# Block-sorted attention and a bilinear feed-forward on one core: Sinkhorn of one batch by itself, Strassen blocks in the out matmul, and a fixed order of work

## The chip, the core and the metric

The kernel runs on one core of a Trainium2 chip. The core has five engines that run side by side, each with its own list of instructions in a fixed order: TensorE (PE, matmuls into PSUM banks), VectorE (DVE), ScalarE (ACT), GpSimd (POOL, which also starts the loads from device memory) and SyncE (SP, which starts stores, transposing transfers and copies through device memory). They wait for one another by semaphores. The metric is device time in microseconds (us) for one execution. Next to it stands the span of a profiled execution, from the first to the last instruction of the core.

## What is computed

There are 4 batches of 8 heads, 768 positions in 8 blocks of 96, head size 64. A small 8x8 matrix per head is normalised five times (exponent, rows, columns; Sinkhorn). It mixes the blocks of k and of v. Attention is then within each block, and its output goes through a bilinear feed-forward: two matrices 512x1536, an elementwise product, a third matrix 1536x512.

```python
P = sort_net                                  # (4, 8, 8, 8)
for _ in range(5):
    P = exp(P - max(P, axis=-1))
    P = P / (sum(P, axis=-1) + 1e-9)
    P = P / (sum(P, axis=-2) + 1e-9)
k_sorted = einsum('bhij,bhjcd->bhicd', P, k_blocks)
v_sorted = einsum('bhij,bhjcd->bhicd', P, v_blocks)
attn = softmax(scale * q_blocks @ k_sorted.T) # inside each block of 96
x = (attn @ v_sorted) as (3072, 512)
out = ((x @ w_a) * (x @ w_b)) @ w_out         # (3072, 512), float32
```

## The kernel before, in words

The matmuls are in bf16 with sums in float32. All work is entered as pieces in a plan (`add` in class `Plan`), each with the engines that may do it, an assumed length, what it depends on, the buffers it takes and returns, and a rank. `solve` walks through assumed time: of the pieces that can begin soonest on an engine it takes the one with the lowest rank, and the result is sorted by assumed start. That sets the order of instructions on each engine for good; on the chip each engine goes through its list and waits where it must.

Two heads make a pair, four pairs a batch. For each pair q is transposed on PE (L473, for batch 3 by a DMA, L625), k and v are mixed with the Sinkhorn matrix on PE (L489, L500 for the halves of batch 0, L537 for v where it goes through device memory, L546 and L550), v is transposed (L559), then scores (L578), exponent on ACT (L583), product with v (L593), division on DVE (L599, L604), and the transposition of the result into `xT` (L612, or a DMA, L620).

The Sinkhorn loop (L413 to L426) works on all 32 heads at once, 32 partitions by 64 numbers: one ACT and six DVE instructions per turn. Its result is repeated 16 times (`p_rep`), transposed by eight small matmuls (L435), and spread with a mask into `s_all` (L440): batch 0 by DVE, the others by POOL. The mixes of a batch wait for its part of `s_all`.

The feed-forward has two stages per batch. The first makes h = (x w_a)(x w_b), transposed. For batch 0 it is plain (L749, 192 matmuls of 384 columns). For batches 1 to 3 it goes by Strassen blocks in Winograd's form (L831): seven products instead of eight, for which POOL and DVE add blocks of the weights (`w_sums`) and of x (`x_sums`), ACT copies a bank between two products that accumulate on it (L840), and DVE or POOL adds and multiplies (L306). The second stage multiplies h by `w_out` (L899): per batch 6 groups of 12 matmuls of 512 columns, each group copied out by ACT (L248) or DVE (L250) and stored by SP (L919). `hT`, `xT` and `tx` exist once; the next batch waits for its readers.

Loads are started by POOL (L350, L362, L379, L387, L406); a load waits for the seventh before it to land. In the beginning PE is kept awake with matmuls on zeros (L983) whose number is worked out from the plan's gaps (`_fill`).

The softmax here doesn't subtract the row's maximum and nothing guards it: scores larger than these inputs give would overflow.

## Time and profile before

| | |
|---|---|
| runs, device time | 245.55, 246.43 and 823.47 us (median 246.43) |
| profiled execution | 245.06 us, span 243.3 us |
| granted TensorE clock | 1.0 |
| matmuls by line, count | L899 288, L831 504, L749 192, L983 48 |
| DMA, mean | 115 GB/s, 27.90 MB; busy from 6 to 62 us nearly without a break |

The page of the profile gives the busy time of each engine, the largest groups of instructions (line, engine, operation, out<-in, partitions x elements, count, busy us, mean ns of one, idle time before it and what ended it), and a chain of work followed back from the last instruction. The chain in order of time shows start, length and what; the timeline shows instructions of one engine, with the idle time before each in brackets. Matmuls overlap, so the spacing of their starts, not the mean length of one, is what one costs in a long run.

### The profile page before, as it was taken

To read this page: it belongs to the slowest core of one execution; us is meant where nothing else is said; L and a number is where in the kernel's file an instruction comes from. 1 tells how busy PE (TensorE), PEld (TensorE's weight loads), DVE (VectorE), ACT (ScalarE), POOL (GpSimd) and SP (SyncE) were. 2 spreads that over 40 slices of the span, in tenths; PEclk is the share of its full clock that TensorE was granted. 3 is DMA by queue.
4 is the path that set the end of the run, shared out by engine and by line. 5 is a ranking of instruction groups with operands and counts; after the bars stand their busy time and mean duration, and the time that the engine had idled before them with its cause. 6 is when DMAs were issued, how large, how long until landed. Compare 5 with 4: busy or idle time off the path is not lost.

```text
span 243.3 us, 5723 instructions
## 1 busy us (share of the span) xinstructions
PE 233.7 (96%) x2204; PEld 132.4 (54%) x2204; DVE 150.1 (62%) x348; ACT 125.3 (52%) x243; POOL 119.6 (49%) x132
## 2 busy tenths in 40 slices
PE   6998999999989999999999999999999999999992
PEld 2466766666655554665544455665654455565440
DVE  6656654654555738589987452988862448886210
ACT  3366646468655533667654443766631076673100
POOL 8979999999970020069755110173540007355000
PEclk9999999999999999999999999999999999999999
DMA  5999999999965683619998867200035450000135
GB/s 67 180 203 187 202 203 187 167 191 178 162 134 107 167 184 78 149 16 154 135 175 110 192 174 178 46 0 0 3 66 108 96 122 0 1 0 3 43 86 129
DMA packets 50106, 27.90 MB, mean 115 GB/s; under 512 B 28832, under 2 KB 47008, under 8 KB 50080
## 3 DMA queue, kind: packets, MB, share of 16 engines
q0 software_dynamic: 24112, 14.16, 43.3%
q1 hardware_dynamic: 25968, 13.38, 25.7%
q8 instruction: 17, 0.28, 0.5%
q14 instruction: 9, 0.07, 0.1%
HBM read 30.29 MB, written 8.26 MB: 158 GB/s over the span
## 4 chain that ended last, share of the span: by engine, by line
PE 67%; ACT 1%; DVE 1%; issue 0%; ACTq 0%; DVEq 0%
PE ps L831 33%; PE ps L899 26%; PE ps L593 2%; PE ps L578 2%; PE ps L489 1%; PE ps L537 1%; PE ps L473 1%; PE ps L749 1%; ACT f L840 0%; DVE xp L604 0%; ACT o L248 0%; DVE a L306 0%; DVE rec L599 0%; ACTq L840 0%; DVEq L306 0%
## 5 line engine op out<-in xcount | busy, mean ns | idle before, releaser
L306 POOL TENSOR_TENSOR hT<-a,f 128x384 bf16<-128x384 bf16 x39 | 35.5, 918 | 78.1 <-DVE f L306 56.3
L899 PE MATMUL ps<-w_out_sb,hT 128*128 128x512 bf16 x288 | 66.4, 379 | 0.0
L840 ACT COPY f<-ps 128x384 f32<-128x384 f32 x108 | 48.2, 482 | 23.6 <-PE ps L831 21.1
L899 PEld LDWEIGHTS <-hT 128*128 128x128 bf16 x288 | 27.0, 98 | 30.1
L306 DVE TENSOR_TENSOR a<-f,ps 128x384 bf16<-128x384 f32 x54 | 29.4, 549 | 10.4 <-PE ps L831 6.4
L306 DVE TENSOR_TENSOR f<-f,ps 128x384 f32<-128x384 f32 x54 | 28.9, 550 | 8.9 <-PE ps L831 6.0
L583 ACT ACTIVATE eT<-ps 96x768 bf16<-96x768 f32 x32 | 24.9, 806 | 17.2 <-PE ps L578 16.9
L306 DVE TENSOR_TENSOR hT<-a,ps 128x384 bf16<-128x384 bf16 x42 | 23.1, 551 | 12.4 <-PE ps L749 6.9
L248 ACT COPY o<-ps 128x512 f32<-128x512 f32 x15 | 8.8, 585 | 36.3 <-PE ps L899 36.3
L831 PE MATMUL ps<-tx,ws_a 128*128 128x384 bf16 x108 | 25.2, 326 | 0.2 <-ACT f L840 0.2
L831 PE MATMUL ps<-tx,ws_b 128*128 128x384 bf16 x108 | 24.9, 326 | 0.3 <-ACT f L840 0.3
L604 DVE TENSOR_TENSOR xp<-ps,rec 96x512 bf16<-96x512 f32 x32 | 21.4, 677 | 0.4
L749 PE MATMUL ps<-xT,w_a_sb 128*128 128x384 bf16 x96 | 19.6, 327 | 0.0
L749 PE MATMUL ps<-xT,w_b_sb 128*128 128x384 bf16 x96 | 19.6, 326 | 0.0
L831 PEld LDWEIGHTS <-ws_b 128*128 128x128 bf16 x144 | 13.8, 98 | 10.1 <-ACT f L840 0.9
L755 ACT CAST a<-ps 128x384 bf16<-128x384 f32 x24 | 11.5, 479 | 14.9 <-PE ps L749 9.1
L250 DVE COPY o<-ps 128x512 f32<-128x512 f32 x9 | 6.2, 691 | 20.8 <-PE ps L899 20.7
L831 PEld LDWEIGHTS <-ws_a 128*128 128x128 bf16 x144 | 13.5, 98 | 10.1 <-ACT f L840 1.4
L831 PE MATMUL ps<-xT,w_b_sb 128*128 128x384 bf16 x72 | 17.6, 326 | 0.3 <-DVE xp L604 0.2
L831 PE MATMUL ps<-xT,w_a_sb 128*128 128x384 bf16 x72 | 17.5, 326 | 0.0
L831 PEld LDWEIGHTS <-w_b_sb 128*128 128x128 bf16 x108 | 10.4, 98 | 7.9 <-DVE xp L604 0.7
L831 PEld LDWEIGHTS <-w_a_sb 128*128 128x128 bf16 x108 | 10.3, 98 | 7.9 <-ACT f L840 0.6
(90 smaller groups left out, 337.9 us busy)
## 6 DMA issues: line engine op xcount, KB each, us to landing
out_dram<-o SPq DMA_DIRECT2D x48, 128.0 KB, 2.4
k<-in_k_dram POOLq DMA_DIRECT2D x16, 192.0 KB, 6.1
v<-in_v_dram POOLq DMA_DIRECT2D x16, 192.0 KB, 6.1
vd<-vm SPq DMA_DIRECT2D x10, 192.0 KB, 2.9
vs<-vd SPq DMA_DIRECT2D x10, 192.0 KB, 3.1
q<-in_q_dram POOLq DMA_DIRECT2D x16, 96.0 KB, 6.9
w_a_sb<-in_moe_w_a_dram POOLq DMA_DIRECT2D x4, 384.0 KB, 7.1
w_b_sb<-in_moe_w_b_dram POOLq DMA_DIRECT2D x4, 384.0 KB, 9.0
```

Of the source, the lines that this page charges most:

```text
L248: nc.scalar.copy(out=out, in_=in_)
L250: eng.tensor_copy(out=out, in_=in_)
L306: ENG[eng].tensor_tensor(out=out, in0=in0, in1=in1, op=op)
L578: nc.tensor.matmul(sc[:, e, i * BLK:(i + 1) * BLK], lhsT=kT[e * D:(e + 1) * D, at:at + P], rhs=rhs, start=True, stop=True)
L583: nc.scalar.activation(out=buf(("eT", b, p, h))[:, :, 0:HB], in_=buf(("sc", b, p, h))[0:BLK, :, 0:HB], func=AF.Exp, scale=float(scale))
L593: nc.tensor.matmul(ops_[:, e, i * OW:(i + 1) * OW], lhsT=eT[:, e, i * BLK:i * BLK + P], rhs=vs[:, h * NBH + i, e * OW:(e + 1) * OW], start ...
L604: nc.vector.tensor_tensor(out=_ap(xp, h * NBH * 2 * D, [[NB * 2 * D, BLK], [D, 2], [2 * D, NBH], [1, D]]), in0=_ap(ops_, 2, [[1024, BLK], ...
L749: nc.tensor.matmul(pf[:, 0:HW], lhsT=w_sb[:, kc, m * P:(m + 1) * P], rhs=buf(("xT", b))[:, kc, t * HW:(t + 1) * HW], start=(kc == 0), stop ...
L755: ea = add("ACT", 0.48, lambda: nc.scalar.copy(out=buf(("a", b, t, m)), in_=buf(("pf", b, t, m, "a"))[:, 0:HW]), [pa], get=[("a", ("a", b, ...
L831: nc.tensor.matmul(buf(key)[:, 0:HW], lhsT=lf(j), rhs=rf(j), start=start and j == 0, stop=j == 1, skip_group_check=not start)
L840: return add("ACT", 0.48, lambda: nc.scalar.copy(out=buf((name, b, g, n)), in_=buf(kA)[:, 0:HW]), [dep], get=[("f", (name, b, g, n))], rank=r)
L899: nc.tensor.matmul(po, lhsT=hT[:, t * 2 + m // G, m % G, c * P:(c + 1) * P], rhs=w_out_sb[:, m, :], start=(m == 0), stop=(m == KO - 1), sk ...
```

## The change

It has five parts.

1. *Sinkhorn of batch 0 by itself.* The 8 heads of batch 0 lie as 64 rows (head and row) of 8 numbers. Row sums are done on TensorE: a float32 matmul against a 0/1 matrix of equal heads (`m_same`) both sums over a head's rows and repeats the sum for each row. The state lies transposed, so that ACT takes the reciprocal of the other sum as its scale, and a turn is one ACT, one PE and three DVE instructions. The last product is laid out so that one matmul (`spread_first`) gives the repeated, transposed matrix. The heads of batches 1 to 3 go through the old loop afterwards (24 partitions), with a lower priority.
2. *Out of batches 2 and 3 by Strassen blocks* (`out_strassen`): three chunks of 128 tokens in each half, seven products of six matmuls of 256 columns each; `o_sums` adds blocks of `w_out` (8 operations, once), 24 sums of blocks of h per batch; ACT copies the accumulating bank three times per chunk, DVE adds four times per chunk and the results are stored. Sums and outputs lie in the buffers of q, k, v, `kT` and `s_all`, free by then. Of the last chunk's stores every second is started by ACT.
3. *Loads in one order.* Each load follows the one entered before it (`ld_i`); q, k, v of batch 0 come first, then the first weight blocks, q's second halves, and the weight blocks 2, 1, 3 instead of 1, 2, 3.
4. *The order of all pieces is given* as a table (`ORDER`, two characters per piece) which `solve` follows in place of its own choice. Assumed lengths and delays in the plan are changed, and POOL and DVE sums are planned as sharing a port.
5. *Weight sums* of the second column block may go to DVE; the filler's zeros lie in a part of `ws_b`.

`PLAIN_G` is 6, equal to `G`, so the feed-forward of batch 0 stays plain.

```diff
+        digits = [c - 35 - (c > 92) for c in ORDER]
+        order = [91 * a + b for a, b in zip(digits[::2], digits[1::2])]
+        def given():
+            op = self.ops[order[done] // 2]
+            e = list(op.alts)[order[done] % 2]
+            return begin(op, e, max(self._when(op), op.ready)), e, op
...
-STRASSEN_OUT = ()
+STRASSEN_OUT = (2, 3)
+PLAIN_G = 6
...
-    warm_sb = const.tile([P, 512], BF16, name="warm_sb")
+    warm_sb = ws_b[:, 3, 1, HW // 2 * 4 - 512:HW // 2 * 4]
...
-        i = add("POOL", 0.72 + many, fn, ds, get=get, rank=rank, lat=0.0)
+        i = add("POOL", 0.72 + many, fn, ds + ld_i[-1:], get=get, rank=rank, lat=0.0)
+        ld_i.append(i)
...
-    for c in range(1, 4):
+    for c in (2, 1, 3):
         load_ab(c)
...
+    def sk_rows():
+        nc.tensor.matmul(buf(bank)[0:HN, NB:2 * NB], lhsT=m_same.rearrange("p h j -> p (h j)"),
+                         rhs=pa[:, 1, :], start=True, stop=True)
...
+    for it in range(4):
+        x = step("ACT", 0.3, lambda it=it: nc.scalar.activation(
+            out=pa[:, 1, :], in_=px if it else buf(bank)[0:HN, 0:NB], func=AF.Exp, scale=pc1), [x], lat=0.2)
+        x = step("PE", 0.12, sk_rows, [x, o_same])
+        x = step("DVE", 0.2, lambda: nc.vector.reciprocal(out=pr, in_=buf(bank)[0:HN, NB:2 * NB]),
+                 [x], put=[bank], lat=0.1)
+        x = step("DVE", 0.2, lambda: stt(px, pa[:, 1, :], 1.0, pr, ps1), [x], lat=0.02)
+        x = step("DVE", 0.15, lambda: nc.vector.reciprocal(out=pc1, in_=ps1), [x], lat=0.1)
...
+    def spread_first():
+        nc.tensor.matmul(buf("p0")[:, 0:HN], lhsT=m_rep.rearrange("p j c -> p (j c)"),
+                         rhs=p_end.rearrange("p i h -> p (i h)"), start=True, stop=True)
...
         last = add("ACT", 0.26, lambda: nc.scalar.activation(out=p_nat, in_=p_nat, func=AF.Exp),
-                   [last], rank=-9)
+                   [last, o_p0], rank=12)
...
+            p1 = pe(kA, h(0, 0), wo(0, 0), False, True, hd(0, 0, late) + [p1], rk - 0.5, gs=late)
+            s1 = snap("os1", p1)
...
+            c11 = plus("os1", kX, 0, 0, [s1, p2], [kX, ("os1", b, c)])
+            p6 = pe(kA, s(1), wt(1), False, True, [s1] + sd(1) + td(1), rk, put=sput(1) + tput(1))
+            u2 = snap("ou2", p6)
+            p5 = pe(kY, s(0), wt(0), True, True, sd(0) + td(0), rk + 0.1, get=[("bank", kY)],
+                    put=sput(0) + tput(0))
+            st["lasty", b] = p5
+            p7 = pe(kA, s(2), wt(2), False, True, [u2] + sd(2) + td(2), rk, put=sput(2) + tput(2))
+            u3 = snap("ou3", p7)
+            p4 = pe(kZ, h(1, 1), wt(3), True, True, [p1, p2] + hd(1, 1) + td(3), rk + 0.6,
+                    get=[("bank", kZ)], put=tput(3))
+            c22 = plus("ou3", kY, 1, 1, [u3, p5], [("ou3", b, c)])
+            c21 = plus("ou3", kZ, 1, 0, [u3, p4], [kZ, ("ou3", b, c), ("och", b, c)])
+            p3 = pe(kY, s(3), wo(1, 1), False, True, [c22] + sd(3), rk, put=sput(3))
+            c12 = plus("ou2", kY, 0, 1, [u2, p3], [kY, ("ou2", b, c), ("och", b, c)])
...
+        if b in STRASSEN_OUT:
+            if wt_ok is None:
+                wt_ok = o_sums(RB - 10.0)
+            out_strassen(b, RB + 40.0, wt_ok)
+        else:
+            for t in range(2):
+                for c in range(3):
+                    out_plain(b, t, c, RB + 40.0)
```

## The prediction

> **What bounds the kernel now.** The page comes first: the span, and the busy time of the engines.
>
> ```profile
> span 243.3 us, 5723 instructions
> PE 233.7 (96%) x2204; PEld 132.4 (54%) x2204; DVE 150.1 (62%) x348; ACT 125.3 (52%) x243; POOL 119.6 (49%) x132
> ```
>
> TensorE (PE) is nearly always busy, but filler matmuls count as busy too. So the chain of waits was read next (start, length, what):
>
> ```profile
> 151.01 0.19 issue
> 151.20 0.21 DVE rec L599
> ...
> 154.50 25.19 PE ps L831 x154
> 179.69 2.16 PE ps L899 x10
> 181.85 0.33 PE ps L831 x2
> 182.17 12.95 PE ps L899 x60
> ...
> 238.70 0.59 ACT o L248
> ```
>
> From 72 us to 238.7 the chain is PE at work, with few breaks, the widest near 118.4, 126.0, 151.0 and 210.8 (0.55, 0.6, 1.2, 1.05 us). A microsecond of PE work removed here is a microsecond off the end, if nothing else is late. An L899 matmul takes 12.95/60 = 0.216 us, an L831 matmul 25.19/154 = 0.164. Third, PE's timeline at the start:
>
> ```profile
> 1.27 4.15 PE L983 MATMUL ps<-warm_sb 128*128 128x512 bf16 x11 [1.27 <-DVE warm_sb L326]
> ...
> 13.47 0.36 PE L435 MATMUL ps<-ident,p_rep 32*128 32x32 bf16 x8
> ...
> 14.42 0.38 PE L500 MATMUL ps<-s_all,k 128*64 128x64 bf16 x12
> ...
> 19.86 0.38 PE L500 MATMUL ps<-s_all,v 128*64 128x64 bf16 x11 [0.99 <-issue]
> ...
> 27.46 0.82 PE L749 MATMUL ps<-xT,w_a_sb 128*128 128x384 bf16 x4
> ```
>
> Until 14.42 PE has little but filler (L983): the Sinkhorn matrix isn't there. Until 27.46 it does batch 0's attention, with breaks; from there it is saturated. Fourth, DVE's timeline of the Sinkhorn loop, whose turns begin 1.75 us apart:
>
> ```profile
> 2.58 0.21 DVE L416 TENSOR_REDUCE rsum<-p_nat 32x8 f32<-32x64 f32 x1
> ...
> 4.33 0.21 DVE L416 TENSOR_REDUCE rsum<-p_nat 32x8 f32<-32x64 f32 x1 [0.32 <-ACT p_nat L414]
> ```
>
> Fifth, groups of instructions on POOL, for a rival (mean ns after the comma):
>
> ```profile
> L306 POOL TENSOR_TENSOR hT<-a,f 128x384 bf16<-128x384 bf16 x39 | 35.5, 918 | 78.1 <-DVE f L306 56.3 <-PE ps L831 21.7
> L306 POOL TENSOR_TENSOR tx<-xT,tx 128x768 bf16<-128x768 bf16 x1 | 1.8, 1831 | 5.4 <-DVE tx L306 5.4
> L306 POOL TENSOR_TENSOR tx<-xT 128x768 bf16<-128x768 bf16 x1 | 1.6, 1632 | 18.2 <-DMA xT<-xp 18.2
> ```
>
> **Part 1: Sinkhorn of batch 0.** The first exponent can still start at 2.29, where sort_net lands. But four small mask operations and the old one now stand ahead of the loop in DVE's order, after the memsets that end near 2.2: 4 x 0.23 (nearest rows 0.21 to 0.25) + 0.34, so DVE is free at 3.4. The opening then needs reciprocal 0.19, product 0.21, matmul 0.17 (mean of one in L435), reduction 0.21, reciprocal 0.19, and some 0.3 of handing over: the first of four turns starts at 4.7. A turn is exponent 0.26, matmul 0.17, three DVE operations 0.19 + 0.21 + 0.19, handing over 0.3: 1.3 us. The matmul is in float32, which the trace lacks; the old turn, 1.75, is the upper bound. PE's order holds up to 2772 filler columns (at 0.216 per 512, 1.17 us) between two of these matmuls, so much below 1.3 is impossible; I take 1.45, nearer the rows. Four turns end at 10.5; last product 0.21, matmul 0.3 with its handing over, first spread 0.42: first mix at 11.4 (10.8 to 12.6) instead of 14.42.
>
> **Part 2: up to the first L749.** Before: 13.04 us (14.42 to 27.46) with 14 mixes (L500) at 0.31, 3 q transposes (L473) 0.31, 5 scores (L578) 0.28, 6 v transposes (L559) 0.27, 5 L593 at 0.26, 4 L612 at 0.19: 10.3 of work, 2.7 lost. After, the order of instructions puts 15, 5, 5, 7, 4, 4 of them there: 11.3, and 0.9 of filler. So 12.2 to 14.0; I take 13.2: first L749 at 24.6. Data bound it from below: v of the last pair lands at 15.5 (issued 8.93, 6.6 us to landing); behind its mix stand 8.4 us of PE work, so not before 24.0. The first w_b block lands at 20.3, hidden. By its first L749 PE has then done one mix, one q and one v transpose more and one L593 less than before (0.31 + 0.31 + 0.27 - 0.26 = 0.6), work that no longer follows. Gain 27.46 - 24.6 + 0.6 = 3.5 us; bounds 1.5 and 4.1.
>
> The Sinkhorn of batches 1 to 3, moved behind, is 5 turns of six DVE operations, 5 x 1.3 = 6.5 us, in DVE's idle time (in 20 to 50 us it is busy 17.9 of 30) among its evictions. It feeds POOL's spread (2.0) for batch 1: after the eight matmuls of its transposition PE's order has 4.6 us before the first batch 1 mix; 0.25 + 0.42 + 2.0 fit. If the covers go, each microsecond late stops PE by as much.
>
> **Part 3: loads.** The first 14 loads and their bytes stay; q now leads, and later ones wait in POOL's queue for one another. POOL has up to the first batch 1 spread 32 loads at 0.73, 6 sums at 1.6, no other spread: 33 us, or by landings (a load waits for the seventh before it) some 39; PE reaches that mix at about 24.6 + 18.7 = 43.3. Cost nothing, cover 2 us. Weight sums half on DVE (8 x 0.55) shorten POOL's list. The extra sort_net issue on SP (0.41) stands before nothing for 60 us.
>
> **Part 4: Strassen in the out stage.** Batches 2 and 3: 144 matmuls of 512 columns (31.1 us) become 252 of 256. Eight 128-column ones with their own 128x128 weights start L559 at 51.12 and end at 51.57: 0.056 each; 384 columns cost 0.164; between them 0.110: 27.7 us, gain 3.4. Below, 256/512 of 0.216 gives 3.9; above, if the halved matmul cost as much as 384 columns, 41.3: a loss of 10. I take 0.110, since weights are already changed with every 128 columns at 0.056.
> Beside it: 48 block sums, 30 on POOL (0.92) and 18 on DVE (half of tx's 0.55, about 0.3), 8 weight sums (6 on DVE, 0.55), 18 ACT snapshots and 24 DVE additions (below 0.48 and 0.55, 384 columns) for 12 evictions. In the two product stages (25.2 and 26.9 us) DVE is busy 21 us, POOL 12; in the out stages DVE 5.5 and 3.6. New waits: the third to seventh products read block sums of the last group, and a snapshot must be copied before the bank accumulates on. Ahead of them stand 5 us of products that need neither (first, second, fourth), and three chunks alternate. The sum chain of the last group (h product 0.56, three sums 0.3, queue before them 2) is 4 to 5 us: just hidden; behind it PE's whole queue, the next batch too. The next batch's first product now also follows the fifth one of the last chunk: order on the same engine, no time. Old breaks (4.2 us in all with 0.78 near 71 us) I leave in.
>
> **Part 5: tail.** From 238.70 the end is 4.6 away: copy 0.59, two store issues (0.55 each), landing 2.4. The last addition is near 0.42 (half-width), and the second store goes by ACT: 0.6 less.
>
> **The sum**, against the profiled execution (245.06 us; span 243.3, 1.76 around it): 245.06 - 3.5 - 3.4 - 0.6 = 237.6. Its runs lie 0.5 and 1.4 above it; with 0.5 I predict 238.1.
>
> **Rivals.**
> *The fixed order fits better than the old list*: the old breaks go too, 4.2 less: 233.9. For it: the breaks are one-off waits. Against: nothing shows the new ones.
> *The start gains nothing*: batch 0's attention is bound by ACT and DVE (7.2 and 7.1 busy of 10 us at 20 to 30) and the stop of 0.99 at 19.86: 241.6.
> *The out stage gives its gain back* to waits on snapshots and sums: 241.5. Both: 245.0.
> *Slower: POOL becomes the bound.* In the last stage its order has 28 operations, 25.7 us at 0.918. First possible 5.5 us into the products (201.40 against 195.9), last needed at 26.9 + 96 x 0.110 = 37.4: room for 32, so it decides from 1.14 us each. Were each twice as long beside a busy DVE, 51.4: 19 us late in each of two batches, 276. For it: tx beside DVE's own tx took 1831 against 1632 ns, 0.2 for an overlap of 0.34. Against: 18 DVE sums are at most 6 us for both batches, 3 each: 28.7 stays below 32. The Trainium skill ("SBUF — State Buffer", section "SBUF: two separate sides") says that a DVE instruction with two SBUF inputs and a GpSimd one that reads SBUF shut each other out for the whole instruction. By it those overlaps would cost their full length, an estimate of up to 3 us of POOL per batch; the 0.2 in 0.34 agrees in part.
>
> **Chances.** Forecast 0.58, better fit 0.14, start 0.10, out stage 0.08, both 0.05, POOL 0.05. A measurement of this kernel tells 2% from no change: faster is below 241.5, slower above 251.4. The single failures lie at that border and are halved: faster 0.58 + 0.14 + 0.09 = 0.81, rounded to 0.79 for the unknown float32 matmul; same 0.15, slower 0.06. Range 234 to 244.5: from the better fit nearly to both failures.
>
> **What would show it.** First mix near 11.4, first L749-like matmul near 24.6; 256-column matmuls 0.110 apart; out stages of batches 2 and 3 near 14 us each without breaks over 0.5; tail 4. Wrong if PE waits for POOL or DVE sums there, for the batch 1 spread near 43, or if the 256-column ones start over 0.13 apart.

## The result, and the profile after

The changed kernel takes 254.08 us (median of 4 runs, 252.71 to 255.74); the kernel before took 246.18 us beside it (median of 4). The ratio is 1.033, 95% interval [1.023, 1.044]: slower, where 238.1 us and a range of 234 to 244.5 were forecast. The profiled execution took 252.71 us, with a span of 250.8 us. In the runs further down the kernel before took 245.1 to 245.6 us (medians), and its profiled execution is the 245.06 us shown above. Ratios leave disturbed runs out, so a ratio can lie a little below the ratio of two medians.

The new lines of the code that the profile names: L1292 filler, L516 and L520 the float32 matmuls of the first Sinkhorn, L551 its spread, L650 half mixes, L639 and L687 mixes, L728 scores, L743 product with v, L754 division, L563 and L568 the two products in a turn of the second Sinkhorn, L588 spread of a batch, L900 plain first stage, L983 Strassen first stage, L1053 plain out, L1146 Strassen out, L391 every sum or product of two tiles.

The page of the profile: span, busy time of the engines, and TensorE's granted clock in 40 slices of 6.3 us, in tenths.

```profile
span 250.8 us, 6043 instructions
PE 235.0 (94%) x2309; PEld 144.9 (58%) x2309; DVE 182.3 (73%) x420; ACT 126.4 (50%) x259; POOL 141.2 (56%) x160
...
PEclk9999689999799999999999999999999999999998
```

PE is busy 1.3 us more than before, and the span is 7.5 us longer. DVE has 32 us more to do and POOL 22. The clock row has two dents in PE's work that were not there before, near 27 and 65 us (the 8 at the end lies behind PE's last matmul). The same in a table by stretches (from:to, length, busy us and number of instructions of PE, its weight load, DVE, ACT and POOL, granted clock, DMA share, GB/s):

```profile
10.00:26.60 16.60, 13.89 (x341) 9.88 (x336) 11.17 (x40) 10.09 (x22) 12.29 (x17) 1.00 1.30 199
26.70:33.40 6.70, 6.70 (x68) 3.97 (x66) 4.33 (x9) 3.37 (x8) 6.65 (x6) 0.50 1.32 204
...
60.00:64.00 4.00, 0.42 (x3) 0.30 (x4) 3.95 (x4) 0.60 (x1) 3.99 (x5) 1.00 1.22 197
64.20:67.60 3.40, 3.40 (x22) 1.65 (x20) 1.05 (x2) 1.28 (x2) 2.46 (x3) 0.50 1.23 191
```

Both dents are stretches at half clock, 6.8 and 3.4 us long, and each follows a stop of PE (one ends at 25.40 us, the other lasts from 59.8 to 63.6). PE's waits over the whole kernel (line, what it waited for, us in total, times, longest; one of 1.2 us ahead of the first filler is left out) name the stops:

```profile
PE ps L687 <- DVE xp L754: 3.8, 1, 3.8
PE ps L650 <- issue: 2.6, 2, 1.9
PE ps L728 <- DVE xp L754: 1.5, 1, 1.5
PE ps L1146 <- DVE v L391: 1.3, 2, 0.8
```

Three of the four are waits for DVE. The fourth, "issue", is one in which PE waits for nothing that the profile shows; PE's timeline puts its two stops in the middle of groups of equal matmuls:

```profile
7.29 2.45 PE L1292 MATMUL ps<-ws_b 128*128 128x512 bf16 x6
...
13.33 0.38 PE L650 MATMUL ps<-s_all,k 128*64 128x64 bf16 x12
...
19.11 0.28 PE L650 MATMUL ps<-s_all,k 128*64 128x64 bf16 x5 [0.74 <-issue]
...
25.40 0.38 PE L650 MATMUL ps<-s_all,v 128*64 128x64 bf16 x11 [1.88 <-issue]
...
29.71 1.46 PE L900 MATMUL ps<-xT,w_a_sb 128*128 128x384 bf16 x4
...
33.87 0.82 PE L900 MATMUL ps<-xT,w_a_sb 128*128 128x384 bf16 x4
```

The first mix comes at 13.33 us (forecast 11.4, before 14.42), the first plain product at 29.71 (forecast 24.6, before 27.46). A filler matmul of 512 columns costs 0.41 us at 7.29, where the kernel before paid 0.216 by then: half speed. The clock row doesn't show this, since the trace's clock record begins only at 9.56 us, with full clock; in the kernel before it begins at 4.55. The spacing of the fillers halves at these same two moments, so they are read here as the moments of full clock. A group of four plain products takes 1.25 us from start to start at 29.71 (the next starts at 30.96) and 0.66 at 33.87, where the clock is full again.

What the waits for DVE are made of is in DVE's timeline, first at 33 us, then at 56:

```profile
33.26 0.19 DVE L562 RECIPROCAL rsum<-rsum 24x8 f32<-24x8 f32 x1
33.49 1.66 DVE L563 TENSOR_TENSOR p_nat<-p_nat,rsum 24x64 f32<-24x64 f32 x1
35.19 0.26 DVE L565 TENSOR_REDUCE csum<-p_nat 24x8 f32<-24x64 f32 x1
35.48 0.19 DVE L567 RECIPROCAL csum<-csum 24x8 f32<-24x8 f32 x1
35.70 1.78 DVE L568 TENSOR_TENSOR p_nat<-p_nat,csum 24x64 f32<-24x64 f32 x1
...
58.46 4.22 DVE L391 TENSOR_TENSOR ws_a<-w_a_sb,ws_a 128x768 bf16<-128x768 bf16 x1
62.61 0.19 DVE L749 RECIPROCAL rec<-ps 96x8 f32<-96x8 f32 x1
62.83 0.69 DVE L754 TENSOR_TENSOR xp<-ps,rec 96x512 bf16<-96x512 f32 x1
```

and in POOL's at the same times:

```profile
33.41 1.65 POOL L391 TENSOR_TENSOR ws_b<-ws_b,w_b_sb 128x768 bf16<-128x768 bf16 x1
...
35.75 1.64 POOL L391 TENSOR_TENSOR ws_b<-w_b_sb,ws_b 128x768 bf16<-128x768 bf16 x1
...
58.60 2.08 POOL L588 TENSOR_TENSOR s_all<-mask,p_col 128x1024 bf16<-128x1024 bf16 x1
60.56 1.70 POOL L391 TENSOR_TENSOR ws_a<-w_a_sb,ws_a 128x768 bf16<-128x768 bf16 x1
```

A product of 24x64 numbers, 0.21 us where POOL is quiet, ends with POOL's weight sum. The reduction and the reciprocal between the two products, with one input each, keep their 0.19 to 0.26 us, but POOL only issues a load at that moment; one_source below has the better comparison. The weight sum on DVE, 0.55 us by itself, takes 4.22: it ends 0.4 us behind POOL's spread and POOL's next sum (2.08 and 1.70). The division that PE waits for comes behind it at 62.83.

The out stage of batch 2 went as forecast, 256-column matmuls 0.109 us apart; in that of batch 3 three sums on DVE meet three on POOL. From the chain of waits (start, length, what):

```profile
189.46 11.24 PE ps L1146 x103
...
231.16 1.64 PE ps L1146 x15
233.56 3.61 DVE v L391 x5
237.31 4.75 PE ps L1146 x42
```

POOL did not become the bound in the form that the rival had. Its products of h keep their length, 929 ns against 918 before:

```profile
L391 POOL TENSOR_TENSOR hT<-a,f 128x384 bf16<-128x384 bf16 x42 | 38.6, 929 | 48.0 <-DVE a L391 34.3
```

**Where the 15 us between forecast and profile lie.** This is an account read from the profile's rows; which of its parts a run confirms, the next section says. The sum of the forecast was 237.6 us for the profiled execution, a span of 235.8. The profile has 250.8. Up to the first plain product 5.1 us: 1.9 for the late first mix, 1.6 for the stops beyond the one of 0.99 that was priced (0.74 + 1.88 - 0.99), 1.5 because the last 3 us before it run at half clock. Between there and the end of PE at 245.6: 1.9 for the rest of the first half-clock stretch, 1.5 + 3.8 for two waits for DVE, 1.7 for the second half-clock stretch, 1.3 for the sums of batch 3; less 1.5 for PE's old waits behind 27.46 (0.8, 0.5 and 0.2 in the kernel before), which the forecast had left in and which are gone. The tail from the end of PE is 5.2 us instead of 4.0. Together 5.1 + 10.2 - 1.5 + 1.2 = 15.0.

### The profile page after: what moved, and what is told of

It reads as the page before. It is cut to its first block, busy times and chain, and to the rows that moved or that the text cites. A ratio compares the mean times of both kernels' runs of the same rounds, so it can differ in the third digit from the quotient of the medians.

```text
span 250.8 us, 6043 instructions
## 1 busy us (share of the span) xinstructions
PE 235.0 (94%) x2309; PEld 144.9 (58%) x2309; DVE 182.3 (73%) x420; ACT 126.4 (50%) x259; POOL 141.2 (56%) x160
## 4 chain that ended last, share of the span: by engine, by line
PE 87%; DVE 7%; issue 3%; ACT 0%; DVEq 0%
PE ps L983 33%; PE ps L1053 13%; PE ps L900 11%; PE ps L1146 10%; PE ps L1292 4%; PE ps L743 3%; PE ps L728 3%; PE ps L623 2%; PE ps L650 2%; PE ps L639 2%; PE ps L687 1%; DVE v L391 1%; PE ps L709 1%; DVE ws_a L391 1%; DVE xp L754 1%
## 5 line engine op out<-in xcount | busy, mean ns | idle before, releaser
L391 POOL TENSOR_TENSOR hT<-a,f 128x384 bf16<-128x384 bf16 x42 | 38.6, 929 | 48.0 <-DVE a L391 34.3
L1053 PE MATMUL ps<-w_out_sb,hT 128*128 128x512 bf16 x144 | 35.0, 380 | 0.0
L391 DVE TENSOR_TENSOR f<-f,ps 128x384 f32<-128x384 f32 x54 | 28.8, 549 | 5.0 <-PE ps L983 2.9
L391 DVE TENSOR_TENSOR a<-f,ps 128x384 bf16<-128x384 f32 x54 | 28.8, 548 | 4.5 <-PE ps L983 3.1
L391 DVE TENSOR_TENSOR hT<-a,ps 128x384 bf16<-128x384 bf16 x42 | 22.9, 551 | 10.2 <-PE ps L900 7.9
L983 PE MATMUL ps<-tx,ws_b 128*128 128x384 bf16 x108 | 25.2, 326 | 0.0
L983 PE MATMUL ps<-tx,ws_a 128*128 128x384 bf16 x108 | 25.1, 326 | 0.0
L754 DVE TENSOR_TENSOR xp<-ps,rec 96x512 bf16<-96x512 f32 x32 | 21.7, 683 | 0.5
L906 ACT CAST a<-ps 128x384 bf16<-128x384 f32 x24 | 11.4, 477 | 19.9 <-PE ps L900 17.8
L900 PE MATMUL ps<-xT,w_a_sb 128*128 128x384 bf16 x96 | 21.0, 350 | 0.0
L900 PE MATMUL ps<-xT,w_b_sb 128*128 128x384 bf16 x96 | 20.7, 342 | 0.0
L1053 PEld LDWEIGHTS <-hT 128*128 128x128 bf16 x144 | 12.8, 98 | 13.3
L983 PEld LDWEIGHTS <-ws_b 128*128 128x128 bf16 x144 | 13.9, 98 | 9.7 <-ACT f L992 0.5
L983 PEld LDWEIGHTS <-ws_a 128*128 128x128 bf16 x144 | 13.9, 98 | 8.9
L983 PE MATMUL ps<-xT,w_a_sb 128*128 128x384 bf16 x72 | 17.3, 326 | 0.0
L983 PE MATMUL ps<-xT,w_b_sb 128*128 128x384 bf16 x72 | 17.2, 326 | 0.0
L321 ACT CAST kT<-ps 128x768 bf16<-128x768 f32 (+1 forms) x18 | 12.3, 693 | 9.1 <-PE ps L639 5.6
L1167 ACT COPY f<-ps 128x256 f32<-128x256 f32 x18 | 6.6, 372 | 19.6 <-PE ps L1146 18.6
L749 DVE RECIPROCAL rec<-ps 96x8 f32<-96x8 f32 x32 | 6.0, 194 | 13.1 <-PE ps L743 12.9
L391 POOL TENSOR_TENSOR tx<-xT,tx 128x768 bf16<-128x768 bf16 x1 | 1.6, 1630 | 22.7 <-DMA vd<-vm 22.7
```

The source lines that it names most:

```text
L321: nc.scalar.copy(out=out, in_=in_)
L391: ENG[eng].tensor_tensor(out=out, in0=in0, in1=in1, op=op)
L754: nc.vector.tensor_tensor(out=_ap(xp, h * NBH * 2 * D, [[NB * 2 * D, BLK], [D, 2], [2 * D, NBH], [1, D]]), in0=_ap(ops_, 2, [[1024, BLK], ...
L900: nc.tensor.matmul(pf[:, 0:HW], lhsT=w_sb[:, kc, m * P:(m + 1) * P], rhs=buf(("xT", b))[:, kc, t * HW:(t + 1) * HW], start=(kc == 0), stop ...
L906: ea = add("ACT", 0.48, lambda: nc.scalar.copy(out=buf(("a", b, t, m)), in_=buf(("pf", b, t, m, "a"))[:, 0:HW]), [pa], get=[("a", ("a", b, ...
L983: nc.tensor.matmul(buf(key)[:, 0:HW], lhsT=lf(j), rhs=rf(j), start=start and j == 0, stop=j == 1, skip_group_check=not start)
```

## The experiments

Theory A at the outset: sums of two tiles on POOL and on DVE hold each other up for as long as both run, and the change puts many of them side by side. Its rivals: the given order doesn't fit the chip; PE's stops and half clock at the start decide; Strassen blocks of 256 columns don't gain what they should.

| run | us, median | ratio to before, 95% |
|---|---|---|
| the change | 254.1 | 1.033 [1.023, 1.044] |
| own_order | 254.0 | 1.035 [1.031, 1.039] |
| own_order_plain_out | 247.5 | 1.010 [1.006, 1.014] |
| less_filler | 257.5 | 1.048 [1.041, 1.055] |
| one_source | 253.9 | 1.033 [1.029, 1.038] |
| last_sums_on_dve | 255.6 | 1.037 [1.030, 1.044] |
| pool_fills | 249.9 | 1.022 [1.013, 1.031] |
| fills_with_loads_first | 247.1 | 1.000 [0.994, 1.005] |
| loads_first | 254.5 | 1.029 [1.020, 1.037] |
| finer_filler | 255.0 | 1.035 [1.027, 1.043] |
| plain_out_pool_sums | 245.4 | 1.001 [0.997, 1.004] |
| plain_out_finer_filler | 245.7 | 0.999 [0.996, 1.002] |
| strassen_pool_weights | 251.3 | 1.024 [1.018, 1.030] |
| strassen_without_block_sums | 242.1 | 0.985 [0.980, 0.989] |
| strassen_dve_sums | 247.0 | 1.006 [1.003, 1.009] |
| strassen_batch3_dve | 246.4 | 1.005 [1.002, 1.008] |
| one_sinkhorn | 253.7 | 1.033 [1.029, 1.038] |
| one_sinkhorn_four_stores | 256.7 | 1.043 [1.036, 1.050] |

### The order, and out by itself

```diff
-ORDER = (...)
+ORDER = b""
```

> The changed kernel without the table of the order: the plan chooses the order itself, with the changed lengths and parts; nothing is left out. The changed kernel takes 254.1 us, the kernel before 246.2. Theory A (four places of the given order lose 17 us of PE time: a late start with a half clock 7, GpSimd holding up DVE's products 1.5, loads behind a spread that waits for PE 5.5, sums of the last batch 4.5): another order has other collisions, so 244 to 250, and the wait of some 4 us near 60 us is gone, since the plan's own ranks put loads before spreads. Theory B (the parts themselves cost more than they save, whatever the order): 252 or more.

Measured 254.0 us: theory B's range. The plan's own list is as slow as the given one, so the table alone is not the cause. The loss lies elsewhere, though. The wait of 3.8 us near 60 us is gone, as theory A said; instead PE waits in the out stage of batch 2 for block sums (1.2 + 1.2 + 0.8 + 0.7 us), which the given order avoids, and two stretches of 3.4 us at half clock follow these waits.

```diff
-STRASSEN_OUT = (2, 3)
+STRASSEN_OUT = ()
```

> As own_order, with the out stage plain for all batches; nothing is left out. 36 matmuls of 512 columns per batch and half against 126 of 256 per batch: PE work alone says 3.4 us longer than own_order. Theory A (sums of blocks wait for GpSimd at the end of the last batch) says that 3 to 5 us of waiting go too: within 2 us of own_order. Theory B (256-column matmuls cost more than forecast): 4 us or more shorter than own_order.

Measured 247.5 us with the plan's own order: the size that theory B named, but not by its reason, since the 256-column matmuls of the change stand 0.109 us apart, as forecast. Out by Strassen blocks thus costs 6.5 us there, where a gain of 3.4 was forecast. The other parts together cost 2.4 where 3.5 were to be gained.

### The start: filler and the products of the second Sinkhorn

```diff
-            rate = 2350.0 if t > 5.0 else 1180.0
+            rate = 2350.0 if t > 12.6 else 1180.0
```

> The changed kernel with filler counted at half the columns until 12.6 us, order as given; nothing is left out. Theory A: filler that runs at half clock until 10 us stands before the float32 matmuls (turns of 2.0 instead of 1.45 us), so the first mix comes at 12 instead of 13.3 and the kernel gains 1 to 3 us: 251 to 253. Rival: with less work TensorE's clock stays at half for longer, batch 0's attention pays for it, and the first matmul with w_a is no earlier than 29.7: 254 to 257.

Measured 257.5 us, on the rival's side (254 to 257). With less filler the turns of the first Sinkhorn come 1.6 us apart instead of 2.0 (float32 matmuls at 5.00, 6.49, 8.07, 9.87) and the first mix at 12.60, but the clock is full only from about 16 us, and PE's one long stop takes 2.6 us. PE also waits 5.0 us in all for v from device memory, so not all of the 3.4 us more is the clock's. Thinner filler made the chain shorter and the start no better (first plain product at 30.38).

```diff
-        last = add("DVE", 0.21, lambda: nc.vector.tensor_mul(
-            out=p_nat, in0=p_nat, in1=...rsum...), [last], rank=12)
+        last = add("DVE", 0.21, lambda: nc.vector.reduce_sum(
+            out=p_nat, in_=...p_nat...), [last], rank=12)
...
```

> The changed kernel; the ten products of the Sinkhorn loop of batches 1 to 3 are replaced by DVE instructions of the same size that read one operand, so the division is left out for these batches (and the exponent is scaled by 0.1); order as given. Theory A (a DVE instruction with two operands in SBUF waits for a whole GpSimd sum): all ten take about 0.2 us instead of 1.7 for three or four of them, PE's wait of 1.5 at 37 us goes, the later spread comes 2 to 4 us sooner: 249 to 252. Rival (DVE's products are slow by themselves, or the wait is of another origin): 253.5 to 254.5, with long instructions still there.

Measured 253.9 us, where theory A had 249 to 252. A line of DVE and one of POOL near 34 us:

```profile
34.48 0.15 DVE L558 TENSOR_REDUCE p_nat<-p_nat 24x64 f32<-24x64 f32 x1
```

```profile
34.34 1.65 POOL L391 TENSOR_TENSOR ws_b<-ws_b,w_b_sb 128x768 bf16<-128x768 bf16 x1
```

With one input from SBUF instead of two, the replaced operations take 0.15 to 0.20 us, beside the same weight sums on POOL too, and PE's wait of 1.5 us at 37 us is gone: it is the second input that makes them wait. So theory A's mechanism holds and its time doesn't: in the profiled execution (256.4 us, the longest of the four) the wait for the division near 60 us is still there with 4.0 us, and 3.1 us of waits for v are new.

### The sums of the given order

```diff
+MOVED = ((3, 2, 5), (3, 3, 3), (3, 3, 0))
...
             e = list(op.alts)[order[done] % 2]
+            if op.tag in MOVED:
+                e = "DVE"
```

> The changed kernel in its given order, with the last three of POOL's block sums of batch 3 given to DVE; nothing is left out. Theory A (a sum on POOL and a sum on DVE hold each other up for as long as both run): the three sums v<-hT that took 1.0 us each on DVE near the end take 0.33 to 0.4, PE's waits after 232 us shrink from about 4.5 to under 2.5 us, and the time falls from 254.1 to about 251.5 us (250.5 to 252.7). Theory B (DVE simply has too much to do behind the last group, whatever POOL does): three more sums of 0.33 to 1.0 us on DVE, so no gain or 1 us more, 254 to 256 us.

Measured 255.6 us: no gain in the time, which lies in theory B's range. In the stage that was touched theory A's mechanism holds. DVE's timeline with the three sums that took 3.06 us in the change:

```profile
238.06 0.89 DVE L394 TENSOR_TENSOR v<-hT 128x384 bf16<-128x384 bf16 x3
```

They take 0.3 us each, and PE has no wait left behind 224 us. But this profile also has a stop of 2.7 us for nothing visible, waits of 3.7 and 2.2 us for the division and 2.8 for v, all before 115 us; these swing from run to run by more than the 2 us that the three sums lost.

```diff
+    def ft(eng, out, in0, in1, op):
+        if eng == "POOL":
+            nc.gpsimd.memset(out, 0.01)
+        else:
+            tt(eng, out, in0, in1, op)
...
-   op.fn = lambda ...: tt(op.eng, s[j], x, y, o)
+   op.fn = lambda ...: ft(op.eng, s[j], x, y, o)
```

The same replacement stands in the sums of `w_out` and of h.

> The changed kernel in its given order, in which POOL's share of the weight sums, of the sums of w_out and of the block sums of batches 2 and 3 is left out: POOL writes a constant to the whole tile instead and reads nothing; DVE's share is computed as before. Theory A (POOL's sums hold up DVE): the products of the second Sinkhorn take about 0.21 us again (1.5 us of PE's wait at 37 us gone), the weight sum on DVE at 58 us still meets the spread of batch 1 (2.1 us) but no second POOL sum, so about 2.3 instead of 4.2 us, and the waits at the end go (4 to 5 us): 254.1 - 1.5 - 1.7 - 4.5 = 246.4 us (244.5 to 249). Theory B (the stops of PE for its program and the half clock of the start decide, the sums lie beside them): 252 to 255 us.

Measured 249.9 us, 4.2 less than the change and 0.9 above theory A's range. DVE's and POOL's timelines near 57 us and near 232, and PE's near 82:

```profile
55.76 1.66 DVE L397 TENSOR_TENSOR ws_a<-ws_a,w_a_sb 128x768 bf16<-128x768 bf16 x1
57.45 0.56 DVE L397 TENSOR_TENSOR ws_a<-w_a_sb,ws_a 128x768 bf16<-128x768 bf16 x1
...
232.17 0.89 DVE L397 TENSOR_TENSOR v<-hT 128x384 bf16<-128x384 bf16 x3
```

```profile
57.67 2.20 POOL L594 TENSOR_TENSOR s_all<-mask,p_col 128x1024 bf16<-128x1024 bf16 x1
59.82 0.73 POOL L392 MEMSET ws_a<- 128x768 bf16 x1
...
232.13 0.77 POOL L392 MEMSET v<- 128x384 bf16 x2
```

```profile
82.14 0.56 PE L749 MATMUL ps<-vs,eT 96*128 96x66 bf16 x8 [2.93 <-DMA vs<-vd]
```

The three block sums that took 3.06 us beside sums on POOL take 0.89 beside constants. The weight sum that took 4.22 us takes 0.56, and the waits for the division and in the last stage are gone. That weight sum owes part of this to luck: it begins 0.22 us ahead of POOL's spread and runs through, where in the change it began 0.14 us ahead and waited. The sum before it takes 1.66 us here and 1.75 in the change, and POOL only issues loads at that time; so loads being issued can hold up DVE too, though in loads_first a sum of the same size took 0.54 beside them. In place of the waits stands one of 2.9 us for v of batch 1, which has been through device memory. PE had no such wait in the change, where it stood hidden behind the one for the division. The next run takes it away.

```diff
+    at = next(i for i, o in enumerate(order) if o.tag == ("spread", 1))
+    late = [o for o in order[at:] if o.tag and o.tag[0] == "load"][:9]
+    rest = [o for o in order[at:] if o not in late]
+    order = order[:at] + late + rest
```

> As pool_fills (the given order; POOL's share of the weight sums and of the out stage's sums is left out, a constant is written; 249.9 us), with nine loads moved in POOL's list ahead of the spread of batch 1, which waits 11 us for the second Sinkhorn: k, v, q of batch 1's last pair, the three of w_out, k, v, q of batch 2's first pair. Theory A (the loads behind that wait come late and PE's 2.9 us wait for v of batch 1 at 82 us is due to them): the DMA gap at 44 to 52 us fills, that wait goes, 249.9 - 2.9 = 247.0 us (246 to 248.3). Rival (that wait comes from the two-way transfer of v through DRAM and the transposes queued with it, not from the loads): 249 to 251 us.

Measured 247.1 us (ten runs, 243.3 to 248.7; the ratio corresponds to 245.5): theory A's 247.0. The loads had been queued on POOL behind a spread that waits 9 to 11 us for the second Sinkhorn; moved ahead of it, they fill the DMA from 44 to 52 us (207 GB/s instead of 2), and the wait for v is gone. By the medians the move is worth 2.8 us, by the ratios 5.6. With POOL's sums left out and the loads moved, 7.0 of the 7.9 us by which the change is slower are gone.

The same move in the change itself, with every sum computed:

> The changed kernel in its given order with nothing left out, and the same nine loads moved in POOL's list ahead of the spread of batch 1. With POOL's sums away this move gave about 3 to 4 us. Theory A (with the sums in, PE's wait of 3.8 us at 60 us is for DVE, whose weight sums stand behind POOL's spread and sums, and the late loads are hidden behind it): 252 to 255 us, no gain that can be measured, and the wait at about 60 us for xp stays unless the spread moves away from DVE's sums. Rival (the loads are late on their own account in the full change as well): 249.5 to 251.5 us.

Measured 254.5 us: no gain clear of the noise (four runs, 250.9 to 255.9), as theory A has it. DVE's timeline near 54 us in this run:

```profile
54.20 4.62 DVE L394 TENSOR_TENSOR ws_a<-w_a_sb 128x768 bf16<-128x768 bf16 x2
```

POOL runs three spreads in a row from 47.47 to 53.39 and then a weight sum to 55.30, two of DVE's weight sums take 4.62 us instead of 1.02, and PE waits 2.9 us behind them; it also still waits 3.2 us for v. The late loads are worth some 3 us or more, but this shows only once the sums no longer hold up DVE.

### PE's stops

```diff
-            n = min(cols, 512)
+            n = min(cols, 256)
```

> The changed kernel in its given order, with the filler cut into matmuls of 256 columns instead of 512: as many columns, nearly twice the filler instructions, so that all later work stands some 50 to 60 instructions further down PE's list. Theory A (PE stops where the next 16 KB of its program must be fetched, at every 256th instruction of its list): the stops that lay in the half mix k of pair 0 (at 18.4 us) and in the half mix v of pair 2 (at 23.5 us) move to earlier work: into the turn of v of pair 2 (L709) and into the half mix v of pair 1 (L650), which come about 2 us sooner; the time stays within 252.5 to 256 us. Theory B (these groups wait for their data, or for a load that lands then): the stops stay at the half mixes of k of pair 0 and of v of pair 2.

Measured 255.0 us. PE's timeline:

```profile
17.84 0.33 PE L709 MATMUL ps<-ident,vT 128*128 128x128 bf16 x3 [1.10 <-issue]
...
24.11 0.25 PE L650 MATMUL ps<-s_all,v 128*64 128x64 bf16 x4 [0.17 <-issue]
...
30.20 0.50 PE L900 MATMUL ps<-xT,w_b_sb 128*128 128x384 bf16 x2 [0.24 <-issue]
```

The stops moved to other work. Among the trace's records of PE (matmuls and weight loads counted) they stand at entry 442, after one of the four transpositions of v, and at entry 694, after eight of the twelve half-mix matmuls: the same two entries as in the change, 252 apart. The third line's stop is at entry 946, again 252 further on. In the other kernels, the one before included, the stops of this kind in the start lie within three entries of 442 and 694. So the place is a property of the list, not of the work that happens to stand there. In both runs the trace has transfers of 16 KB on an instruction queue shortly ahead of the stops (at about 16.9 and 23.1 us in the change). That PE waits for more of its list to arrive fits this, but no run shows it. The length of a stop is another matter: 0.74 and 1.88 us in the change, 1.10 and 0.17 here, 0.99 and none in the kernel before.

### Weight sums out of the way

```diff
-            al = (("POOL", 1.75), ("DVE", 0.55)) if c == 1 else (("POOL", 1.75),)
+            al = (("POOL", 1.75),)
-                d = [w_in[n, c], w_in[n, c + 2]]
+                d = [w_in[n, c], w_in[n, c + 2], o_col]
```

with `STRASSEN_OUT = ()`, `ORDER = b""` and the rank of the second column block as that of the first.

> The plan's own order, all of out in plain form, and all sixteen weight sums on POOL and only after the second Sinkhorn has ended; nothing is left out. The same with DVE's share and free times took 247.5 us. Theory A (the sums met the products of the second Sinkhorn and cost PE 1.67 + 0.69 us of waits there): 247.5 - 2.4 = 245.1 us (244 to 246.3), that is level with the kernel before. Rival: the sums now come late and the first Strassen block of batch 1 waits for them, or the sums meet other work on DVE: 247.5 to 252 us.

Measured 245.4 us, level with the kernel before, as theory A said: the weight sums that met the second Sinkhorn cost 2.1 us. (The edit moves them in time and off DVE at once; which of the two counts it doesn't tell.) The finer filler on top:

> The run with out in plain form and all weight sums on POOL (245.38 us), with the filler cut into matmuls of 256 columns, which moves PE's later work some 50 to 60 instructions down its list; nothing is left out. Theory A (what is left of the start's loss is PE's stops at every 256th instruction and the half clock that follows the long one, and the place of the stops decides their length, 1.1 and 0.2 us instead of 1.2 and 2.1): 245.4 - 2.0 = 243.4 us (242 to 245), that is faster than the kernel before. Rival (the stops hide behind the loads that batch 1 waits for): 245 to 246.5 us.

Measured 245.7 us: the rival. The list moved, but a stop of 2.2 us and a half-clock stretch of 6.8 us came up at another place.

### Strassen out, its sums kept, left out, and moved

The run plain_out_pool_sums with `STRASSEN_OUT = (2, 3)` again:

> The plan's own order, out of batches 2 and 3 by Strassen blocks with their sums, all sixteen weight sums on POOL after the second Sinkhorn; nothing is left out. With out in plain form this took 245.38 us. Theory A (Strassen out costs 6.5 us, whatever the weight sums do): 245.4 + 6.5 = 251.9 us (250 to 253.5). Rival (its cost came from meeting the weight sums, or from the clock of the start): under 249 us.

Measured 251.3 us, as theory A had it: 5.9 us more than with plain out. PE's waits:

```profile
PE ps L1111 <- POOL v L356: 2.1, 3, 0.9
...
PE ps L1111 <- DVE o L356: 1.2, 1, 1.2
...
PE ps L1111 <- POOL k L356: 1.1, 2, 0.9
PE ps L1111 <- DVE v L356: 0.7, 1, 0.7
```

5.1 us in front of the block products, all for sums or for DVE work that stands behind sums. The plan had put 41 of the 56 sums on POOL.

The same with the sums left out:

```diff
-                op = add((("DVE", 0.33), ("POOL", 0.92)), None, None,
+                continue
...
-            return lambda g: buf(("wt", j, g // 3))[:, g % 3 * HD:(g % 3 + 1) * HD]
+            return wo(j % 2, j // 2)
...
-                return lambda g, cs=cs: sb(j, g)[:, cs]
+                return h(j // 2, j % 2)
```

> As the run with all weight sums on POOL and Strassen blocks for out of batches 2 and 3, but the 48 block sums of h and the 8 sums of w_out are left out: the block products read plain blocks of h and of w_out in their place (output not the reference's). PE, ACT's snapshots and DVE's additions are the same. Theory A (PE's gain is real and the sums are the cost): 245.4 - 3.4 = 242.0 us (241 to 243.7). Theory B (the narrow products, the snapshots or the chain of additions are the cost, or the half clock): 247 us or more.

Measured 242.1 us, theory A's 242.0: 3.3 us under plain out. So the gain on PE that was forecast (3.4) is real, and the 56 sums cost 9.2 us.

With all sums computed, but on DVE alone:

```diff
-                op = add((("DVE", 0.33), ("POOL", 0.92)), None, None,
+                op = add((("DVE", 0.33),), None, None,
```

and the sums of `w_out` likewise.

> As the run with all weight sums on POOL and Strassen blocks for out of batches 2 and 3, but all 48 block sums and 8 sums of w_out are put on DVE, at 0.3 and 0.55 us each; POOL keeps only its products hT<-a,f there; nothing is left out. Theory A (it is the meeting of sums on POOL with work on DVE): DVE has some 13 us more to do over the last 80 us but is not held up by POOL's sums: 245 to 249 us. Theory B (the number of sums is too large for DVE at whatever speed): 250 to 256 us, with PE waiting for DVE's sums in front of the block products.

Measured 247.0 us, inside theory A's range, so more sums on the busier engine cost 4.2 us less than fewer. (POOL has less to do in this run as well; the meeting itself is read from the timelines.) The timeline near 186 us:

```profile
185.75 6.48 POOL L356 TENSOR_TENSOR tx<-xT 128x768 bf16<-128x768 bf16 x1 [4.22 <-DMA xT<-xp]
...
186.62 0.88 DVE L356 TENSOR_TENSOR v<-v,hT 128x384 bf16<-128x384 bf16 x3
...
187.61 0.49 PE L1111 MATMUL ps<-q,k 128*128 128x256 bf16 x3 [1.79 <-issue]
```

Here it is POOL that stands still: one sum, 1.63 us by itself, takes 6.48 while DVE runs some 20 short ones. PE's 1.79 us end when DVE has the last sum of the kind that the products need (the line of the trace says "issue"); batch 2's sums come in one heap, since their buffers come free only with the attention of batch 3.

The same for batch 3 alone:

```diff
-STRASSEN_OUT = (2, 3)
+STRASSEN_OUT = (3,)
```

> The plan's own order, all weight sums on POOL after the second Sinkhorn, out by Strassen blocks for batch 3 alone, its block sums and the sums of w_out on DVE alone; nothing is left out. With batches 2 and 3 this took 247.03 us and PE waited 0.8 + 1.8 us for the heap of batch 2's sums. Theory A (only that heap and POOL's sums spoil it; in batch 3 the sums come group by group): 245.4 - 1.7 = 243.7 us (242.8 to 244.8), faster than the kernel before. Rival (in batch 3 too DVE's sums hold up POOL's products or PE): 245 us or more.

Measured 246.4 us: the rival's time, but not for its reason. PE has no wait in the last stage. DVE's last line and SP's last store:

```profile
239.15 0.42 DVE L356 TENSOR_TENSOR s_all<-f,ps 128x256 f32<-128x256 f32 x1 [0.23 <-PE ps L1111]
```

```profile
242.08 0.55 SPq L1174 DMA_DIRECT2D out_dram<-s_all  x1
```

From the last addition's end (239.57) to the end of the span (245.5) it is 5.9 us; in the kernel before, from the end of the last copy (239.29 to 243.3), 4.0. Plain out stores one group of rows every 2.6 us; by blocks all outputs of batch 3 are complete only in the last 4 us, and their stores queue up. The tail gives back 1.9 us, which is about the gain (1.7).

### One Sinkhorn again

The loop of the kernel before for all 32 heads, in the place of both, and the rest as in plain_out_pool_sums.

> The run with out in plain form and all weight sums on POOL (245.38 us), with the Sinkhorn of the kernel before put back: one for all four batches, row sums on DVE, first mix after it; the order of the loads and the rest stay; nothing is left out. Theory A (the split brings the first mix forward by about 1 us, and PE's stops for its program and the half clock in the stretch of small matmuls take it back, so it is worth nothing): 244.5 to 246.5 us. Rival (the split is worth the 3.5 us that were forecast, and something else in the new load order or plan loses them): 247 to 249.5 us. A third case (the split costs more at the start than it gives): under 244.3 us.

Measured 253.7 us, beyond both theories. PE waits 5.0 us for v of batch 2 at 102 us, and half clock follows; in its list on SP the transfer of the last pair stands behind more output stores than it did. The first plain product comes at 29.32 us, as with the split (28.5 to 30.8 in the other runs). Once more, with as many store tiles as the changed kernel has:

> As one_sinkhorn (out in plain form, all weight sums on POOL, one Sinkhorn for all four batches as in the kernel before), with four store tiles as in the changed kernel and the spread columns held in one of them; nothing is left out. Theory A (the split Sinkhorn is worth nothing by the first plain product of batch 0, since PE's stops and the half clock take it back): first such product at 29 to 30 us as with the split (29.4 to 30.1), and, if no other wait appears, 244.5 to 246.5 us. Rival (the split is worth 3.5 us): first such product at 31.5 us or later, 247 us or more.

Measured 256.7 us. The same wait of 4.9 us is there, and this time the first plain product comes at 33.23, behind stops of 0.8 and 2.2 us. The two profiles contradict each other about the start, so theory A isn't shown. With the wait (5 us) and its half-clock stretch (1.7) taken off both, 247.0 and 250.0 would be left against 245.4 with the split. That is an argument and no measurement: what the split by itself is worth stays open, and so does what the order of the loads and the changed lengths are worth, which no run takes out alone.

## Why the prediction was wrong, point by point

**Part 1, first mix at 11.4: 13.33.** The step that failed is the filler between the float32 matmuls, priced at full clock (0.216 per 512 columns). In the change full clock came only at 9.56 us, the filler cost 0.41 until then, and the turns came 2.0 us apart on the mean (float32 matmuls at 5.00, 6.98, 9.67, 11.09). Where the clock was full early, as in last_sums_on_dve, they stood 1.36, 1.49 and 1.99 apart and the first mix came at 12.03, inside the range that was given; the last gap is ACT, where a copy of q, late by a wait for q's load, stands ahead of the exponent. "Much below 1.3 is impossible" and 1.45 were right for the first two gaps at full clock; that full clock could come as late as 10 us was not weighed. Nor is the clock all of it. Six profiles with the split Sinkhorn had full clock by 5.5 us, and only two of them a first mix in the range: in three others PE waited 1.2 to 1.4 us for q's load ahead of it, and the mix came at 12.80, 12.84 and 13.30. The prediction put no wait for q there.

**Part 2, first plain product at 24.6: 29.71.** The count of the work was right: 24.6 + 1.9 for the mix + 1.6 for the stops + 1.5 for half clock is 29.6. In strassen_without_block_sums, where the clock was full from 4.75 us on, 24.6 + 1.9 (the mix, late by the wait for q) + 2.4 (stops of 1.5 and 1.9 instead of 0.99) = 28.9 stands against a measured 28.82. The stop of 0.99 us in the trace of before had been read as one event with its own price. It was the visible one of a kind that comes every 252 entries of PE's list (442, 694 and, in finer_filler, 946). The prediction carried it over, and didn't ask where the next one would fall.

**The second Sinkhorn "in DVE's idle time", its turns at 1.3 us.** This failed. Idle time was there, but at those moments POOL ran weight sums: products took 1.66 to 1.78 us instead of 0.21. one_source shows that the second input makes the difference, plain_out_pool_sums that the weight sums there cost 2.1 us in the plan's own order.

**Part 3, "cost nothing" and "weight sums half on DVE shorten POOL's list".** Both failed. The weight sums on DVE met POOL's spread and sums (4.22 us instead of 0.55) and held up a division that PE waited for: 3.8 us and a half-clock stretch of 3.4. Behind that stood the loads queued after the spread, worth some 3 us or more (fills_with_loads_first against pool_fills) and invisible until the first was gone. The cover of 2 us had been worked out for PE's first mix of batch 1; what else is queued behind the waiting spread on POOL was not followed.

**Part 4, gain 3.4 at 0.110 per matmul: right.** 0.109, and 3.3 us with the sums left out. The sum chain, "just hidden", was mis-sized. Three sums of 0.3 us took 3.06 us beside three on POOL, and PE waited 1.3. In the given order PE shows no other wait for them, and by the account above most of the gain stayed; in the plan's own order, with 41 sums on POOL, it cost 9.2 us.

**Part 5, tail 0.6 shorter: failed.** 5.2 us instead of 4.0, since the outputs of the last batch are complete all at once.

**The rivals.** "The start gains nothing" (241.6) was too mild: it lost 1.6 us (29.71 against 27.46, less the 0.6 of work done earlier). "Slower: POOL becomes the bound" had the right mechanism at the wrong place and price. It asked whether POOL's list fits into the last stage (it does, 929 ns each), and priced the lock at "up to 3 us of POOL per batch". The price lay on DVE, whose operations PE waits for, and in the stage where POOL had its longest instructions, 1.65 to 2.1 us. The Trainium skill's page "SBUF — State Buffer", section "SBUF: two separate sides", says that the one who starts first keeps the shared port for the whole instruction. The runs agree on the whole instruction and go further: DVE's sum waited through two of POOL's instructions (4.22 us), and POOL's through some 20 of DVE's (6.48 us). On who starts first they are not plain: by the trace DVE's sum began 0.14 us before POOL's spread, and it was DVE that waited. The evidence in the trace of before, 1831 ns against 1632 for one overlap, was taken as agreeing "in part"; that overlap, of 0.34 us, was too short to show the size.

**The break-even.** The plain fix (plain out, weight sums on POOL after the second Sinkhorn) is level with the kernel before: 0.9967 to 1.0043. No version that computes everything beat it.

## What to carry to other kernels

Before an elementwise operation with two inputs in SBUF is moved onto DVE or POOL, list what the other of the two runs at that moment; if that also reads SBUF, price the move by the length of the other's instruction, several times over if it has a row of them, and ask which engine waits for the result. A wait that is taken away uncovers the next: products, weight sums and late loads lay behind one another here, and each of one_source and loads_first, tried alone, measured as nothing clear of the noise. Work that PE saves at the very end of a kernel is only worth something if the stores can follow; results that all complete together wait for the DMA.

## What the runs showed of the hardware

PE's stops for nothing visible fall in the start at fixed entries of its list, 252 apart, and cost 0.2 to 2.7 us each, whatever work stands there. In 16 of the 18 profiles with such a stop of 1.1 us or more the granted clock went to half by 1.5 us after one of them, for 3.4 or 6.8 us and once for 10.2 (one_sinkhorn_four_stores); in the two others it didn't (strassen_without_block_sums, with stops of 1.5 and 1.9 us, and one_sinkhorn, with 1.8 and 0.9). Full clock came at 4.4 to 5.5 us or between 7 and 11 in kernels whose first 10 us are nearly the same, and at 16.2 with the thinner filler. The Trainium skill's page "TensorE: Matmul & The Clock Gate", Part 1, describes an activity window of some 3.4 us that runs freely; the lengths, all multiples of 3.4 us, and the swing from run to run agree with that. The stops ahead of them were shorter than such a window. It means that a stop's price is not its length alone: half of the stretch that follows, 1.7 or 3.4 us and once 5.1, comes with it where PE is busy throughout.
